# Row-tiled q projection, a VectorE maximum and reciprocal, and one set of PSUM banks in a fused linear-attention and MoE kernel

## The chip, the cores and the metric

The kernel runs as one program on one core of a Trainium2 chip. The metric is the device time of one execution in microseconds. The kernel before takes 699.37 us (median of 3 runs, 699.26 to 699.45). The output must match the reference.

## The reference

Linear attention over 8 batches, 8 heads, 576 tokens and a head size of 64, with 128 random features. Its output, 4608 tokens of 512 values, goes through a feed-forward layer with a softmax-weighted unit and a layer norm.

```python
def _attn_ref(q, k, v, w_phi):
    def phi(x):
        proj = np.einsum('bhsd,df->bhsf', x, w_phi)
        proj = proj - np.max(np.abs(proj), axis=-1, keepdims=True)
        return np.concatenate([np.exp(proj), np.exp(-proj)], axis=-1)
    q_p, k_p = (phi(q), phi(k))
    kv = np.einsum('bhsf,bhsd->bhfd', k_p, v)
    z = np.sum(k_p, axis=2)
    num = np.einsum('bhsf,bhfd->bhsd', q_p, kv)
    den = np.einsum('bhsf,bhf->bhs', q_p, z)[..., None] + 1e-06
    return (num / den).astype(np.float32)

def _moe_ref(x, w_in, w_out, g_ln):
    h = x @ w_in
    e = np.exp(h - np.max(h, axis=-1, keepdims=True))
    sm = e / (np.sum(e, axis=-1, keepdims=True) + 1e-09)
    solu = h * sm
    mu = np.mean(solu, axis=-1, keepdims=True)
    var = np.mean((solu - mu) ** 2, axis=-1, keepdims=True)
    ln = (solu - mu) / np.sqrt(var + 1e-06) * g_ln
    return (ln @ w_out).astype(np.float32)
```

## The kernel before

**Units.** The attention runs in 16 units, one for each batch and each half of the heads (`u`, two units to a batch). A unit has two halves (`sub`), each a pair of heads `j` = 0, 1. For a half the kernel projects k to features (`pjk`), takes the row maximum (`m`), subtracts it (`dk`), takes both exponentials (`ek`) and accumulates keys times values into one PSUM bank (`kv`, 40 matmuls). The features of q come out with features on partitions, in fp32 as `fq`. `num` (36 matmuls) multiplies them with `kv`, and ScalarE copies the result, numerator and denominator together, into `E`. `den_recip` (line 741) and `divide` finish the half with `rc`, `xn` and `xm` on GpSimd.

**q.** Units 0 to 2 project q plainly in fp32 (`pjq`, then transposes `dT`). The other 13 units, 26 halves, take the path that the change rewrites. `q_load` (line 632) loads q of a pair with its 64 rows twice, so that 128 partitions hold it twice (576 KB). `q_hi` rounds all of it to the fast fp32 format on ScalarE, and `q_lo` lets GpSimd overwrite the lower 64 partitions with the rounding remainder, so that one 128-row operand `hq` holds the high part above the low part. `q_proj` (line 644) projects a head and a chunk (320 or 256 tokens) with two full-height matmuls, one with the high weights in both halves (`w_hh`) and one with the low weights above zeros (`w_l0`). A half has four such steps. VectorE transposes each result in blocks of 32 (`blk`), and `q_max4` takes the maximum over 32 features. The maximum over the four partition groups then goes round the engines: a PE transpose (`mtp`), a VectorE maximum (`mt`), a GpSimd copy (`mb`), a PE transpose back (`mcp`), a ScalarE copy (`mcol`). GpSimd subtracts it (`blk<-blk,mcol`), VectorE transposes back into another tile (`pT`) and ScalarE takes the exponentials.

**MoE.** 36 tiles of 128 tokens. For each, a turned copy of the tokens comes through DRAM (`xB`, `dx`, `xT`), is split into high and low (`mxh`, `mxl`), and 24 matmuls fill the two banks of `h`. VectorE takes the maximum (`nm`), ScalarE the exponential, VectorE the product (`eu`), and the result is turned through DRAM (`ub`, `du`, `uTs`), split (`uhs`, `uls`) and multiplied by the output weights (24 matmuls `o`). These weights are unpacked, scaled and centred (`wraw`, `w`, `cms`, `win_l`, `w_out_l`) while the first units run.

**Order.** Every step is one entry of a list, and a table of numbers, `SEQUENCE`, gives the order in which all of them are issued. Each engine carries out its own share strictly in that order. Buffers and PSUM banks are handed out first in, first out along the same order. The eight PSUM banks are three `a` (attention), one `kv`, two for one `h`, and two `mo` (MoE outputs, and `pjk` and `pjq` of early units). From tile 31 on (`TAIL_T`) the attention banks are closed and reopened as a second `h` and two more output banks (`start_tail`, line 1102).

**Where the listing says L263.** The engine wrapper records all instructions at one line, so the profile is read by tile names.

Of the kernel before, what the change touches and what calls it, by code (L numbers as in the profile page):

```python
# [1218 lines left out]
```

## Time and profile before

| what | value |
|---|---|
| median of 3 runs | 699.37 us (699.26 to 699.45) |
| profiled execution, its own time | 699.55 us |
| span of that execution, first to last instruction | 697.8 us |
| mean granted TensorE clock | 0.987 of full speed |
| TensorE (PE) busy | 664.7 us, 95% |
| VectorE (DVE) busy | 472.2 us, 68% |
| GpSimd (POOL) busy | 455.5 us, 65% |
| ScalarE (ACT) busy | 365.1 us, 52% |
| DMA moved | 110.75 MB, 159 GB/s |

PE is the TensorE matmul stream, PEld its weight loads, which lie beside it. Busy time is the union of an engine's instructions. Since matmuls are pipelined, what a matmul costs the stream is the distance from its start to the next one's start, and not its duration. The 1.75 us between span and time lie outside the instructions.

### The profile page before, as it was taken

The page shows a single profiled execution, that of the slowest core. Times are in us where ns is not written, and L with a number is a line of the kernel's source. Part 1 is how long each engine was busy: PE and PEld are TensorE (multiplying, and loading weights), DVE is VectorE, ACT ScalarE, POOL GpSimd, SP SyncE. Part 2 cuts the span into 40 slices and gives each one's busy share as a digit, 9 for nine tenths or more (in the row PEclk, how much of TensorE's full clock was granted, in tenths as well). Part 3 has the DMA queues.
Part 4 walks back from the last instruction along what each step waited for, and adds up shares of the span by engine and source line. Part 5 has one row for each costly group of instructions (what it writes and reads, how often), then busy time and mean ns, then how long its engine had stood idle before and what let it go on. Part 6 is the DMA issues. An engine that isn't in the chain of part 4 may idle for free.

```text
span 697.8 us, 18768 instructions
## 1 busy us (share of the span) xinstructions
PE 664.7 (95%) x7618; PEld 561.0 (80%) x7618; DVE 472.2 (68%) x737; ACT 365.1 (52%) x674; POOL 455.5 (65%) x488
## 2 busy tenths in 40 slices
PE   5968799889999999999999999999999999999998
PEld 4866678778888888888878888888788888788887
DVE  6999788756677786685668577667756773366420
ACT  3967467436564636464656374635644665232232
POOL 1149878986798467766894769754868485553541
PEclk9899899999999999999999999999999999999999
DMA  8954354645465556447544456556555533255342
GB/s 263 355 144 135 90 170 161 150 137 170 128 168 157 173 188 165 147 161 215 179 130 144 96 187 180 154 144 193 165 175 166 173 109 100 71 189 191 104 146 76
DMA packets 109222, 110.75 MB, mean 159 GB/s; under 512 B 46672, under 2 KB 85840, under 8 KB 108624
## 3 DMA queue, kind: packets, MB, share of 16 engines
q1 hardware_dynamic: 109136, 109.55, 51.7%
q8 instruction: 60, 0.98, 0.6%
q14 instruction: 26, 0.21, 0.1%
HBM read 72.29 MB, written 37.22 MB: 157 GB/s over the span
## 4 chain that ended last, share of the span: by engine, by line
PE 73%; POOL 10%; DVE 7%; DMA 4%; issue 2%; SPq 2%; ACT 1%; POOLq 0%; ACTq 0%; DVEq 0%
PE h L263 25%; PE o L263 22%; PE num L263 8%; PE kv L263 8%; PE pjk L263 4%; PE pq L263 4%; DVE w L263 3%; POOL rc L263 3%; POOL hq L263 2%; SPq L263 2%; POOL uls L263 2%; POOL xn L263 1%; DMA rawq<-in_q 1%; DMA wraw<-in_w_in 1%; DVE m L263 1%
## 5 line engine op out<-in xcount | busy, mean ns | idle before, releaser
L263 ACT ACTIVATE ek<-dk 128x512 f32<-128x512 f32 (+1 forms) x160 | 87.6, 585 | 47.8 <-DVE dk L263 47.0
L263 PE MATMUL o<-w_out_h,uhs 128*128 128x512 f32 x280 | 112.3, 401 | 0.0
L263 PE MATMUL o<-w_out_l,uhs 128*128 128x512 f32 x280 | 109.4, 391 | 0.0
L263 PE MATMUL o<-w_out_h,uls 128*128 128x512 f32 x280 | 109.3, 391 | 0.0
L263 POOL TENSOR_TENSOR uls<-uTs,uhs 128x1024 fp32r<-128x1024 f32 x35 | 83.7, 2393 | 31.3 <-ACT uhs L263 23.5
L263 PE MATMUL h<-win_h,mxh 128*128 128x512 f32 x288 | 92.3, 402 | 1.3 <-DVE eu L263 1.2
L263 PE MATMUL h<-win_h,mxl 128*128 128x512 f32 x288 | 89.1, 391 | 0.2 <-POOL mxl L263 0.2
L263 PE MATMUL h<-win_l,mxh 128*128 128x512 f32 x288 | 89.3, 391 | 0.0
L263 POOL TENSOR_TENSOR mxl<-xT,mxh 128x512 fp32r<-128x512 f32 x36 | 46.4, 1289 | 60.6 <-ACT mxh L263 41.9
L263 DVE TENSOR_REDUCE nm<-h 128x1 f32<-128x1024 f32 x36 | 43.8, 1217 | 59.0 <-PE h L263 59.0
L263 POOL TENSOR_TENSOR hq<-rawq,hq 64x1152 fp32r<-64x1152 f32 x26 | 70.5, 2711 | 20.2 <-ACT hq L263 15.4
L263 PEld LDWEIGHTS num<-kvf,fq 128*64 128x64 f32 x2304 | 72.7, 142 | 9.4 <-issue 3.5
L263 PE MATMUL kv<-rv,ek 128*64 128x65 f32 x2048 | 76.9, 222 | 0.8 <-issue 0.8
L263 PE MATMUL num<-kvf,fq 128*64 128x65 f32 x2304 | 77.3, 227 | 0.0
L263 ACT ACTIVATE fq<-pT 128x512 f32<-128x512 f32 (+1 forms) x104 | 66.5, 679 | 19.4 <-DVE pT L263 15.2
L263 DVE STREAM_TRANSPOSE blk<-pq 128x320 f32<-128x320 f32 (+1 forms) x104 | 45.4, 461 | 41.3 <-PE pq L263 37.4
L263 PEld LDWEIGHTS kv<-rv,ek 128*64 128x64 f32 x2048 | 70.9, 138 | 2.2 <-issue 2.2
L263 POOL TENSOR_TENSOR blk<-blk,mcol 128x1152 f32<-128x1152 f32 x26 | 55.5, 2135 | 19.5 <-ACT mcol L263 17.3
L263 ACT ACTIVATE eu<-h,nm 128x1024 f32<-128x1024 f32 x36 | 40.2, 1116 | 51.3 <-DVE nm L263 51.2
L263 DVE TENSOR_REDUCE m<-pjk 128x4 f32<-128x512 f32 (+1 forms) x80 | 48.7, 625 | 24.8 <-PE pjk L263 24.7
L263 PEld LDWEIGHTS h<-win_h,mxl 128*128 128x128 f32 x288 | 53.9, 188 | 12.5 <-POOL mxl L263 0.6
L263 PEld LDWEIGHTS h<-win_l,mxh 128*128 128x128 f32 x288 | 54.1, 188 | 12.0
(93 smaller groups left out, 1326.4 us busy)
## 6 DMA issues: line engine op xcount, KB each, us to landing
du<-ub SPq DMA_DIRECT2D x35, 512.0 KB, 2.9
uTs<-du SPq DMA_DIRECT2D x140, 128.0 KB, 3.3
rawq<-in_q SPq DMA_DIRECT2D x26, 576.0 KB, 4.8
dx<-xB SPq DMA_DIRECT2D x36, 256.0 KB, 2.8
xT<-dx SPq DMA_DIRECT2D x144, 64.0 KB, 2.6
out<-os SPq DMA_DIRECT2D x35, 256.0 KB, 2.8
rawk<-in_k SPq DMA_DIRECT2D x32, 256.0 KB, 3.7
rv<-in_v SPq DMA_DIRECT2D x32, 256.0 KB, 4.1
```

Source lines behind the costliest of these rows:

```text
L263: return self.tc.keep_in_program_order(method(*args, **kwargs))
```

## The change

The q path of the 26 halves is rewritten. q is loaded once (a pair of heads on 128 partitions, 288 KB); high and low parts are two tiles `hq` and `lq`. The projection of a chunk is one step of six matmuls for both heads: three products (high weights with high q, low weights with high q, high weights with low q), each as two matmuls on 64 rows of the array, head 0 on the upper and head 1 on the lower rows, into two banks. The maximum over the partition groups is made by seven small VectorE instructions through one PSUM tile (`far`, named `m4p` in the order). The transposes back are in place. The sum with epsilon moves to ScalarE (`den_eps`), the reciprocal to VectorE. The separate bank sets and the reopening for the tail go: there are five `a` banks, `kv` and one `h`. Buffers of q are regrouped (`qr`, `qh`, `q4`), `xt` has three in place of four. `SEQUENCE` is a new table; its numbers are left out.

```diff
-    rk=3, rkm=2, rv=3, m=4, d=3, e=5, eh=2, kf=2, q4=5, m4=2, mt=2, mb=2, E=2, rc=2,
-    xn=2, xm=2, xt=4, m2k=5, big=8, nm=2, sm=3, bst=2, mv=2, sa=2, sc=3,
+    rk=3, rkm=2, rv=3, m=4, d=3, e=5, eh=2, kf=2, qr=2, qh=4, q4=3, m4=2, E=2, rc=2,
+    xn=2, xm=2, xt=3, m2k=5, big=8, nm=2, sm=3, bst=2, mv=2, sa=2, sc=3,
...
-PSUM_BUFS = dict(a=3, kv=1, h=1, mo=2)
-TAIL_BUFS = dict(th=1, tmo=2)
+PSUM_BUFS = dict(a=5, kv=1, h=1)
...
-        st["rq", sub] = sb("q4", [P, 2, S], name="rawq")
+        st["rq", sub] = sb("qr", [P, S], name="rawq")
...
-        hq = st["hq", sub]
-        hi_lo_sub(nc.gpsimd, hq[D:], st["rq", sub][D:], hq[D:])
-
-    def q_proj(st, sub, j, c):
-        pq = bank("a", [P, 512], "pq")
-        n = QC[c]
-        x = st["hq", sub][:, j, Q0[c] : Q0[c] + n]
-        nc.tensor.matmul(pq[:, :n], lhsT=w_hh, rhs=x, start=True, stop=False)
-        nc.tensor.matmul(pq[:, :n], lhsT=w_l0, rhs=x, start=False, stop=True)
-        st["pq", sub, j, c] = pq
+        st["lq", sub] = sb("qh", [P, S], F32R, "lq")
+        hi_lo_sub(nc.gpsimd, st["lq", sub], st["rq", sub], st["hq", sub])
+
+    def q_proj(st, sub, c):
+        pq = st["pq", sub, c] = two_banks("pq")
+        n, cs = QC[c], slice(Q0[c], Q0[c] + QC[c])
+        hq, lq = st["hq", sub], st["lq", sub]
+        for i, (w, x) in enumerate(((w_hh, hq), (w_ll, hq), (w_hh, lq))):
+            for j, r in enumerate(HEADS):
+                nc.tensor.matmul(pq[j][:, :n], lhsT=w[r, :], rhs=x[r, cs], start=i == 0, stop=i == 2)
...
+        far = bank("a", [P, 512], "m4p")
+        m = st["m4", sub] = sb("m4", [P, NM])
...
+        nc.vector.tensor_copy(out=far[:64, :NM], in_=m[64:])
+        nc.vector.tensor_tensor(out=m[:64], in0=m[:64], in1=far[:64, :NM], op=ALU.max)
+        nc.vector.tensor_copy(out=far[:32, NM : 2 * NM], in_=m[32:64])
+        for q in (3, 2, 1, 0):
+            out = m[32 * q : 32 * q + 32]
+            nc.vector.tensor_tensor(out=out, in0=m[:32], in1=far[:32, NM : 2 * NM], op=ALU.max)
...
-            nc.vector.transpose(out=st["pt", sub][:, j, cs], in_=blk[:, j, cs])
+            nc.vector.transpose(out=blk[:, j, cs], in_=blk[:, j, cs])
...
+    def den_eps(st, sub):
+        st["rc", sub] = sb("rc", [P, 9], name="rc")
+        nc.scalar.activation(out=st["rc", sub], in_=st["E", sub][:, :, 0], func=AF.Copy, bias=EPS)
+
     def den_recip(st, sub):
-        rc = st["rc", sub] = sb("rc", [P, 9], name="rc")
-        nc.gpsimd.tensor_scalar(out=rc, in0=st["E", sub][:, :, 0], scalar1=EPS, scalar2=None, op0=ALU.add)
-        nc.gpsimd.tensor_tensor(out=rc, in0=rc, in1=neg_one, op=ALU.pow)
+        nc.vector.reciprocal(out=st["rc", sub], in_=st["rc", sub])
...
-    def start_tail():
-        nonlocal psa
-        att_stack.close()
-        psa = ctx.enter_context(tc.tile_pool(name="pst", bufs=1, space=PSUM))
```

The order on TensorE behind one visit (`num` and `kv`) in the middle of the program, before. `pq` is the q projection, `mtp` the transpose of the maximum, `h` the first MoE product, `pjk` the projection of k; rows with x2 or x8 are that many matmuls.

```order
L263 MATMUL pq<-hq,w_hh 128x320
L263 MATMUL pq<-hq,w_l_77 128x320
L263 MATMUL mtp<-ident,m_2888 36x128
L263 MATMUL h<-win_h,mxh 128x512 x2
L263 MATMUL h<-win_l,mxh 128x512 x2
L263 MATMUL h<-win_h,mxl 128x512 x2
L263 MATMUL h<-win_h,mxh 128x512 x2
L263 MATMUL h<-win_l,mxh 128x512 x2
L263 MATMUL h<-win_h,mxl 128x512 x2
L263 MATMUL pjk<-wph,rawk 128x128 x8
```

A like place behind a visit in the order after, on the same engine:

```order
L250 MATMUL pq<-hq,w_hh 128x320 x2
L250 MATMUL pq<-hq,w_ll 128x320 x2
L250 MATMUL pq<-lq,w_hh 128x320 x2
L250 MATMUL pjk<-wph,rawk 128x128 x8
L250 MATMUL h<-win_h,mxh 128x512 x2
L250 MATMUL h<-win_l,mxh 128x512 x2
L250 MATMUL h<-win_h,mxl 128x512 x2
L250 MATMUL h<-win_h,mxh 128x512 x2
L250 MATMUL h<-win_l,mxh 128x512 x2
L250 MATMUL h<-win_h,mxl 128x512 x2
```

The projection of a chunk now stands as six matmuls in a row, each row here being the pair for the two heads, and no `mtp` stands in front of `h`.

The order on VectorE around one maximum, before (`m_2888` is the maximum over 32 features, `pT` the transposes back of another half, `ub` and `bst` work of MoE tiles):

```order
L263 BN_AGGR mv<-bst 128x2
L263 TENSOR_REDUCE m_2888<-blk 128x36
L263 STREAM_TRANSPOSE pT<-blk 128x256 x2
L263 TENSOR_REDUCE mt<-mtp 36x32
L263 STREAM_TRANSPOSE ub<-eu 128x8x4x32
L263 TENSOR_REDUCE m<-pjk 128x4 x2
```

And around one maximum after:

```order
L250 TENSOR_REDUCE m_2294<-blk 128x36
L250 COPY m4p<-m_2294 64x36
L250 TENSOR_TENSOR m_2294<-m_2294,m4p 64x36
L250 COPY m4p<-m_2294 32x36
L250 TENSOR_TENSOR m_2294<-m_2294,m4p 32x36 x4
L250 STREAM_TRANSPOSE blk<-pq 128x320
L250 TENSOR_REDUCE nm<-h 128x1
```

The seven small instructions stand in one run behind the large maximum, where before one `mt` came after other work.

The order on GpSimd ahead of the first MoE tile, before, from the fourth division (`rc`, `xn`, `xm`) to the first `mxl`; `win_l` is the low part of the input weights:

```order
L263 TENSOR_SCALAR rc<-E 128x9
L263 TENSOR_TENSOR rc<-rc,neg_one 128x9
L263 TENSOR_TENSOR xn<-E,rc 128x4x128
L263 TENSOR_TENSOR xm<-E,rc 64x64 x2
L263 TENSOR_TENSOR win_l<-w_3_736,win_h 128x1024
L263 TENSOR_TENSOR win_l<-w_0_233,win_h 128x1024
L263 TENSOR_TENSOR win_l<-w_2_1064,win_h 128x1024
L263 TENSOR_TENSOR mxl<-xT,mxh 128x512
```

The same place after:

```order
L250 TENSOR_TENSOR xn<-E,rc 128x4x128
L250 TENSOR_TENSOR xm<-E,rc 64x64 x2
L250 TENSOR_TENSOR win_l<-w_2_959,win_h 128x1024
L250 TENSOR_TENSOR win_l<-w_1_259,win_h 128x1024
L250 TENSOR_TENSOR win_l<-w_3_644,win_h 128x1024
L250 TENSOR_TENSOR mxl<-xT,mxh 128x512
```

The two `rc` rows of the division are gone from GpSimd; three `win_l` and the first `mxl` stand behind the fourth division as before.

## Rows read from the trace of the kernel before

**Rows 1.** The page, part 1: busy us, share of the span, instructions of each engine.

```profile
PE 664.7 (95%) x7618; PEld 561.0 (80%) x7618; DVE 472.2 (68%) x737; ACT 365.1 (52%) x674; POOL 455.5 (65%) x488
```

**Rows 2.** Busy time by stretch: start:end, length, then each engine's busy us; clock, DMA.

```profile
0.00:88.00 88.00, 66.65 (x1140) 56.78 (x1140) 75.74 (x102) 55.47 (x115) 45.15 (x50) 0.90 0.63 196
88.00:188.00 100.00, 95.09 (x1122) 79.56 (x1124) 71.41 (x113) 57.33 (x109) 81.57 (x80) 1.00 0.53 153
188.00:600.00 412.00, 409.70 (x4929) 347.09 (x4924) 281.77 (x468) 224.94 (x410) 290.27 (x307) 1.00 0.53 157
600.00:697.80 97.80, 93.28 (x437) 77.52 (x435) 43.25 (x56) 27.31 (x41) 38.47 (x53) 1.00 0.41 137
```

**Rows 3.** The page, part 4: the chain that ended last, share of the span by engine.

```profile
PE 73%; POOL 10%; DVE 7%; DMA 4%; issue 2%; SPq 2%; ACT 1%; POOLq 0%; ACTq 0%; DVEq 0%
```

**Rows 4.** Timeline of PE, 204 to 212 us: start us, duration us, instruction, count.

```profile
204.47 0.30 PE L263 MATMUL pq<-hq,w_l 128*128 128x320 f32 x1
204.61 0.27 PE L263 MATMUL mtp<-ident,m 128*36 128x128 f32 x1
204.64 0.71 PE L263 MATMUL h<-win_h,mxh 128*128 128x512 f32 x2
205.19 0.62 PE L263 MATMUL h<-win_l,mxh 128*128 128x512 f32 x2
205.64 0.62 PE L263 MATMUL h<-win_h,mxl 128*128 128x512 f32 x2
...
207.00 0.61 PE L263 MATMUL h<-win_h,mxl 128*128 128x512 f32 x2
207.55 1.16 PE L263 MATMUL pjk<-wph,rawk 64*128 64x128 f32 x16
208.64 0.73 PE L263 MATMUL h<-win_h,mxh 128*128 128x512 f32 x2
209.21 0.62 PE L263 MATMUL h<-win_l,mxh 128*128 128x512 f32 x2
...
211.61 0.28 PE L263 MATMUL pq<-hq,w_l 128*128 128x256 f32 x1
211.73 0.27 PE L263 MATMUL mcp<-ident,mb 128*128 128x128 f32 x1
```

**Rows 5.** Groups by line and form: count, busy us, mean ns, idle before.

```profile
L263 PE MATMUL pq<-hq,w_hh 128*128 128x320 f32 x52 | 18.7, 360 | 3.0 <-DVE dk L263 1.8 <-POOL sa L263 1.1
...
L263 PE MATMUL mtp<-ident,m 128*36 128x128 f32 x26 | 7.0, 275 | 1.1 <-DVE dk L263 0.6 <-DVE m L263 0.4
```

**Rows 6.** Timeline of the weight loads (PEld) of that `pjk` at 207.55 us.

```profile
207.55 0.97 PEld L263 LDWEIGHTS pjk<-wph,rawk 64*128 64x128 f32 x16 [0.35 <-issue]
```

**Rows 7.** Groups by line and form of VectorE and GpSimd: count, busy us, mean ns.

```profile
L263 POOL TENSOR_TENSOR hq<-rawq,hq 64x1152 fp32r<-64x1152 f32 x26 | 70.5, 2711 | 20.2 <-ACT hq L263 15.4 <-issue 2.1 <-POOL blk L263 1.3
L263 POOL TENSOR_TENSOR rc<-rc,neg_one 128x9 f32<-128x9 f32 x32 | 59.6, 1861 | 2.7
...
L263 DVE SCALAR_TENSOR_TENSOR w<-wraw,w 128x1024 uint32<-128x1024 uint32 x16 | 24.7, 1549 | 0.1
...
L263 DVE TENSOR_REDUCE mt<-mtp 36x32 f32<-36x128 f32 x26 | 6.8, 260 | 10.3 <-PE mtp L263 10.2
```

**Rows 8.** Timeline of DVE, one of the shortest instructions and the next.

```profile
212.86 0.21 DVE L263 BATCH_NORM_AGGREGATE mv<-bst 128x2 f32<-128x12 f32 x1
212.99 1.17 DVE L263 TENSOR_REDUCE nm<-h 128x1 f32<-128x1024 f32 x1
```

**Rows 9.** Timeline of DVE ahead of the first `h`; in brackets the idle time before.

```profile
76.22 0.71 DVE L263 STREAM_TRANSPOSE xB<-xn 128x512 f32<-128x512 f32 x1 [2.25 <-POOL xn L263]
...
80.57 2.05 DVE L263 SCALAR_TENSOR_TENSOR w<-wraw,w 128x1024 uint32<-128x1024 uint32 x1
```

**Rows 10.** Timeline of PE from the first `h` on.

```profile
88.08 0.70 PE L263 MATMUL h<-win_h,mxh 128*128 128x512 f32 x2
...
96.27 1.50 PE L263 MATMUL warm<-mb 128*128 128x128 f32 x12
```

More of the change, by code (lines that the diff above doesn't have):

```diff
@@ L298, in bank @@
     def bank(tag, shape, name):
-        pool = psa if tag in ("a", "kv", "th", "tmo") else ps
-        return pool.tile(shape, F32, tag=place(tag), bufs=1, name=name)
+        return ps.tile(shape, F32, tag=place(tag), bufs=1, name=name)
     def hi_lo_sub(eng, lo, full, hi):
@@ L309, in linear_attention_then_moe @@
     w_hh = const.tile([P, F], F32R, name="w_hh")
-    w_l0 = const.tile([P, F], F32R, name="w_l0")
-    mb_tiles = [const.tile([P, 4, 32], F32, name=f"mb{i}") for i in range(SBUF_BUFS["mb"])]
+    w_ll = const.tile([P, F], F32R, name="w_ll")
+    zero = const.tile([P, P], F32, name="zero")
     win_h = const.tile([P, DM // P, DF], F32R, name="win_h")
@@ L325, in linear_attention_then_moe @@
     neg_half = work.tile([P, 1], F32, tag="neg_half", bufs=1, name="neg_half")
-    neg_one = work.tile([P, 9], F32, tag="neg_one", bufs=1, name="neg_one")
     make_identity(nc, ident)
     nc = Engines(tc)
-    nc.vector.memset(mb_tiles[0], 0.0)
+    nc.vector.memset(zero, 0.0)
     for t in v_half:
@@ L338, in linear_attention_then_moe @@
     nc.gpsimd.memset(neg_half, -0.5)
-    nc.gpsimd.memset(neg_one, -1.0)
-    nc.gpsimd.memset(w_l0.bitcast(F32), 0.0)
-    for t in mb_tiles[1:]:
-        nc.gpsimd.memset(t, 0.0)
     w_out_tiles = {}
@@ L361, in warm @@
     def warm():
-        z = mb_tiles[0].rearrange("p a b -> p (a b)")
-        w = bank("mo", [P, 512], "warm")
+        w = bank("a", [P, 512], "warm")
         for _ in range(NWARM):
-            nc.tensor.matmul(w[:, :P], lhsT=z, rhs=z, start=True, stop=True)
+            nc.tensor.matmul(w[:, :P], lhsT=zero, rhs=zero, start=True, stop=True)
     def phi_weights():
@@ L428, in w_mean @@
     def w_mean():
-        cm = bank("mo", [P, DM], "cmean")
+        cm = bank("a", [P, DM], "cmean")
         for c in range(2):
@@ L456, in linear_attention_then_moe @@
     op("set", "gpsimd", 1150, -9e4, lambda: None)
-    op("warm", "tensor", NWARM * mm32(P), -1e5, warm, alloc=[("mo", "warm")])
+    op("warm", "tensor", NWARM * mm32(P), -1e5, warm, alloc=[("a", "warm")])
     op("wp", "sync", dma(16 * D * F, True), -40, phi_load)
     op("phi", "scalar", 200, -20, phi_weights, (), ["wp"])
-    op("phil", "vector", 200, -20, phi_weights_lo, after=["phi"])
+    op("phil", "vector", 400, -20, phi_weights_lo, after=["phi"])
     op("gain", "sync", (475, 450), 5, g_load)
@@ L510, in v_half_load, with two_banks @@
         st["vz"] = vz
-    def two_banks(tag, name):
-        if tag == "h":
-            pj = bank(tag, [P, DF], name)
-            return [pj[:, 512 * j : 512 * (j + 1)] for j in range(2)]
-        return [bank(tag, [P, 512], name) for _ in range(2)]
+    def two_banks(name):
+        return [bank("a", [P, 512], name) for _ in range(2)]
     def by_rows(x, pj):
@@ L526, in by_rows, with by_block, k_rows, k_mid @@
                 )
-    def by_block(x, tag, name):
-        pj = bank(tag, [P, 512], name)
+    def by_block(x, name):
+        pj = bank("a", [P, 512], name)
         nc.tensor.matmul(pj[:, : 2 * F], lhsT=x[:, :P], rhs=wph, start=True, stop=True)
         return pj
-    def k_rows(st, g, tag):
-        st["pj", g] = two_banks(tag, "pjk")
+    def k_rows(st, g):
+        st["pj", g] = two_banks("pjk")
         by_rows(st["rk", g], st["pj", g])
-    def k_mid(st, tag):
-        st["pj", 1] = {None: by_block(st["rk", 1], tag, "pjk")}
+    def k_mid(st):
+        st["pj", 1] = {None: by_block(st["rk", 1], "pjk")}
     def row_max(m, pj):
@@ L695, in q_sub @@
         nc.gpsimd.tensor_tensor(
-            out=blk, in0=blk, in1=st["mc", sub].unsqueeze(2).to_broadcast([P, NM, 32]), op=ALU.subtract
+            out=blk, in0=blk, in1=st["m4", sub].unsqueeze(2).to_broadcast([P, NM, 32]), op=ALU.subtract
         )
     def q_back(st, sub, c):
-        if c == 0:
-            st["pt", sub] = sb("q4", [P, 2, S], name="pT")
         blk = st["blk", sub].rearrange("p j b f -> p j (b f)")
@@ L710, in q_exp @@
         nc.scalar.activation(
-            out=st["qf", sub, c][:, :, s, :], in_=st["pt", sub][:, :, Q0[c] : Q0[c] + QC[c]],
+            out=st["qf", sub, c][:, :, s, :], in_=st["blk", sub].rearrange("p j b f -> p j (b f)")[:, :, Q0[c] : Q0[c] + QC[c]],
             func=AF.Exp, scale=1.0 - 2.0 * s,
@@ L791, in add, with banks @@
                [(tag, x[1] if x[0] == "abs" else (u, *x)) for tag, x in alloc], q(tiles), early)
-        def bank_of(tag, g, j):
-            return 0 if tag == "h" or j is None else j
-        def banks(tag, name, g):
-            return [(tag, (name, g, x)) for x in sorted({bank_of(tag, g, j) for j in heads_of(g)})]
+        def banks(name, g):
+            return [("a", (name, g, j)) for j in heads_of(g)]
         heads_of = lambda g: (None,) if g == 1 else (0, 1)
@@ L888, in linear_attention_then_moe @@
-                add(("qmc", sub), "tensor", mm(128), z + 0.7, q_mc, (sub,), [("qmb", sub)], [("a", ("mcp", sub))],
-                    [("mb", sub)])
-                add(("qml", sub), "scalar", 90, z + 0.8, q_mcol, (sub,), [("qmc", sub)], [("m4", ("mc", sub))],
-                    [("mcp", sub)])
-                add(("qs", sub), "gpsimd", 2070, z + 1, q_sub, (sub,), [("qml", sub)], (), [("blk", sub), ("mc", sub)])
+                for c in range(2):
+                    add(("qp", sub, c), "tensor", 3 * (QC[c] / 2.4 + 12), z - 1.2 + 0.4 * c, q_proj, (sub, c),
+                        [("qlo", sub), ("abs", "phil")], [("a", ("pq", sub, c, j)) for j in range(2)],
+                        [("hq", sub), ("lq", sub)])
+                    for j in range(2):
+                        add(("qt", sub, c, j), "vector", dve(QC[c]) + 27, z - 1.0 + 0.4 * c + 0.2 * j, q_turn, (sub, j, c),
+                            [("qp", sub, c)] + prev, () if prev else [("q4", ("blk", sub))],
+                            [("pq", sub, c, j), ("blk", sub)])
+                        prev = [("qt", sub, c, j)]
@@ L893, in linear_attention_then_moe @@
+                add(("qm4", sub), "vector", dve(2 * S) + 800, z, q_max, (sub,), prev,
+                    [("m4", ("m4", sub)), ("a", ("m4p", sub))], [("blk", sub)])
+                add(("qs", sub), "gpsimd", 2070, z + 1, q_sub, (sub,), [("qm4", sub)], (), [("blk", sub), ("m4", sub)])
             for c in range(2):
@@ L900, in linear_attention_then_moe @@
                             [("qe", sub, c, 0)] if s else [("qb", sub, c)], () if s else [("e", ("f", sub, c))],
-                            [("pt", sub), ("f", sub, c)])
+                            [("blk", sub), ("f", sub, c)])
                 else:
@@ L939, in linear_attention_then_moe @@
     M = {}
-    tail = lambda t: t >= TAIL_T
-    turn_tag = lambda t: "q4" if t > LAST else "big"
     def moe_xturn(t):
@@ L971, in moe_lo, with moe_h @@
         hi_lo_sub(nc.gpsimd, lo, M["src", t], hi)
-    def moe_h(t, half, tag):
+    def moe_h(t, half):
         xh, xl = M["xh", t], M["xl", t]
         if half == 0:
-            M["h", t] = bank(tag, [P, DF], "h")
+            M["h", t] = bank("h", [P, DF], "h")
         h = M["h", t]
@@ L1041, in moe_uls, with moe_t @@
         hi_lo_sub(nc.gpsimd, lo, full, hi)
-    def moe_t(t, i, tag):
-        M["uT", t, i] = bank(tag, [P, 4, P], "uT")
+    def moe_t(t, i):
+        M["uT", t, i] = bank("a", [P, 4, P], "uT")
         for c in range(4):
@@ L1062, in moe_o @@
         if half == 0:
-            M["o", t] = bank("mo", [P, DM], "o")
+            M["o", t] = bank("a", [P, DM], "o")
         o = M["o", t]
@@ L1070, in linear_attention_then_moe, with moe_o_last @@
     LAST = 33
-    def moe_o_last(t, half, tag):
+    def moe_o_last(t, half):
         uh, ul = M["uh", t], M["ul", t]
-        o = M["o", t, half] = bank(tag, [P, DM], "o")
+        o = M["o", t, half] = bank("a", [P, DM], "o")
         cs = slice(half * 256, half * 256 + 256)
@@ L1100, in moe_od @@
         nc.sync.dma_start(out=out[t * P : (t + 1) * P, :], in_=M["os", t])
-    def start_tail():
-        nonlocal psa
-        att_stack.close()
-        psa = ctx.enter_context(tc.tile_pool(name="pst", bufs=1, space=PSUM))
-    op("tail", "gpsimd", 0, 2 * B * UNIT + 40, start_tail, (),
-       [(2 * B - 1, "qv", s, c) for s in range(2) for c in range(2)] + [(2 * B - 1, "kve", 1)])
     for t in range(NTOK // P):
@@ L1114, in linear_attention_then_moe @@
         n = lambda k, *a: ("moe", t, k, *a)
-        te = ["tail"] if tail(t) else []
-        h_tag = "th" if tail(t) and t % 2 else "h"
-        u_tag = "tmo" if tail(t) else "mo"
-        e_tag = "e" if tail(t) else "big"
+        e_tag = "e" if t > 30 else "big"
         op(n("xt"), "vector", 640, z - 20, moe_xturn, (t,), dep, [("xt", n("xB"))], xs)
```

126 lines of the change are left out of this document (39 added, 87 removed), and 250 rows, old and new, of the table SEQUENCE.

## The prediction

> **What bounds the kernel now.** I began with the page's first part [rows 1]: TensorE is busy for 664.7 of 697.8 us, so 33 us at most are lost there, and no other engine is over 68%. The stretches [rows 2] tell where. Up to 88 us, just before the first MoE matmul [rows 10], TensorE is busy for 66.65 us and idle for 21.4. VectorE is the fullest engine there, 75.74 of 88 us, because the weights are unpacked there. From 88 to 188 us TensorE idles 4.9 us, from 188 to 600 us 2.3, and after 600 us 4.5, most of it behind the last matmul. The chain [rows 3] agrees: 73% of the span on TensorE, 10% on GpSimd, 7% on VectorE. So from 88 us on an edit is worth what it takes from the matmul stream, unless the stream then waits for VectorE or GpSimd. Before 88 us it is worth what it takes from VectorE's and GpSimd's path to the first `h`.
>
> All sums below are made against the profiled span of 697.8 us. The execution's own time was 699.55 us, 1.75 more; the median of the runs is 0.18 less than that.
>
> **q projection on TensorE: −6.8 us.** What a matmul costs is the distance to the next start. A 320-column step costs 0.14 us (204.47 to 204.61) and a 256-column one 0.12 (211.61 to 211.73) [rows 4]. A half has four of each kind, so 4 × 0.14 + 4 × 0.12 = 1.04 us, and 52 groups like the one in [rows 5] make 26 halves of two chunks and two heads. After, a half has twelve matmuls in six pairs, three pairs for each width. If the two of a pair run at once on the two halves of the array, a pair costs what a single costs now: 3 × 0.14 + 3 × 0.12 = 0.78 us. That saves 0.26 × 26 = 6.8 us. Does a pair run at once? The trace has no 64-row matmul in the fast format, but it has 64-row ones in fp32: `pjk` issues 16 records of 128 columns in 1.09 us (207.55 to 208.64), 0.068 each [rows 4], against at most 1.50 / 12 = 0.125 for the full-height fp32 records of the same size, `warm` [rows 10]. So pairs overlap nearly fully there, and I take that. The other end is no overlap, 2 × 0.78 = 1.56 us a half, which is +0.52 × 26 = +13.5 us (a rival below).
>
> **PE transposes of the maximum gone: −6.2 us.** `mtp` itself moves the next start by only 0.03 us (204.61 to 204.64), but the pair of `h` behind it takes 0.55 us (204.64 to 205.19) where a pair takes 0.45 (205.19 to 205.64) [rows 4]. So one transpose costs 0.12 to 0.13; there are 26 `mtp` [rows 5] and as many `mcp`: 52 × 0.12 = 6.2 us.
>
> **More changes between row-tiled and other matmuls: +2.8 us.** Going from `h` to `pjk` the last pair takes 0.55 us (207.00 to 207.55), 0.10 over 0.45 [rows 4]. The projection now is a 64-row one and so has such joints, where the full-height one had none towards `h` and `o`. Counting every joint between 64-row, 64-column and full matmuls down the two orders gives 136 before and 164 after: 28 × 0.10 = 2.8 us. Several projections stand next to `pjk` or a visit, where a joint exists anyway. The first pair of `h` after `pjk` takes 0.57 us (208.64 to 209.21), another 0.12; if the projection leaves that behind too, it is 28 × 0.22 = 6.2 us. The low end is 0.
>
> **The warm-up moved: −1.3 us.** The six dummy matmuls `warm` stand at 96.27 us, behind the first `h` tile, and take 1.50 us of the stream [rows 10]; 0.1 of that is the overlap with what follows, which I put at −1.3. In the new order they stand ahead of the first visit, where TensorE waits anyway. Cover gone, they cost the same 1.3 again.
>
> **VectorE: +28 us of work, at no cost as long as it is covered.** The trace has no 36-column instruction on VectorE. The nearest are `mv`, whose next instruction starts 0.13 us later (212.86 to 212.99) [rows 8], and `mt`, 0.26 [rows 7]. Seven of them are 0.9 to 1.8 us; I take 0.15 each, near `mv`, which is the smaller and reads what was just written, as these do: 1.05 us, less the 0.18 of the `mt` that goes, × 26 = +23 us. The 32 reciprocals at 0.15 are +5 us. The Trainium skill, VectorE: DVE Perf Modes, section on the TRN2 errata, speaks against this edit: each instruction pays a fixed latency, some 150 cycles as measured there, so many small ones pay it many times. By that, 7 × (150 + 36) / 0.96 GHz = 1.36 us a half, an estimate from the page, and +31 us for the maxima; no row here shows a chain of this kind. What hides the work: VectorE is at 71.41 of 100 us and 281.77 of 412 [rows 2], so it goes to some 76 to 79%. What queues behind the seven are `nm` and `eu`, which free the only `h`, and the transposes `blk`, which free the projection's banks. The tightest place is the stretch from the first `h` to the seventh: adding spacings row by row, the new order holds 79 us of VectorE work against 91 us of matmuls, where the old one holds 68 against 94. I price the extra waiting there and later at +3 us, somewhat under half of what TensorE idles now from 88 to 600 us, 4.9 + 2.3 = 7.2 us [rows 2]. The bounds are −4 (the waits for GpSimd in the next part go, and nothing comes) and +12.
>
> **GpSimd and ScalarE: relief, worth 3 us in the head.** `rc` takes 1.86 us, 32 times, and its addition about 0.3: 70 us go. The remainder of q goes from 2.71 us at 1152 columns [rows 7] to about half that, 26 × 1.3 = 34 us, and `mb` with 7 us. GpSimd falls from 455 to about 345 us. The round trip of a maximum over TensorE, GpSimd and ScalarE no longer exists, so `blk<-blk` on GpSimd waits for VectorE alone. ScalarE loses half of `hq` and `mcol` and gains 32 additions. In the steady part GpSimd was not the bound, and I count its relief inside the +3 above. In the head it was on the path: at 76.22 us VectorE waited 2.25 us for GpSimd's `xn`, which stood behind `rc`, and the last unpacking step took 2.05 us [rows 9] where the mean of its kind is 1.55 [rows 7]. The new order has the same matmuls ahead of the first `h` (53 us by their spacings, both orders) and the same VectorE work (69 and 70 us). So the first `h` comes earlier by what GpSimd held up. I take −3 us; the bounds are −7 (wait and slow steps both gone) and +3 (two more small maxima and reciprocals in the way, keys loaded before queries).
>
> **Banks, tail, loads.** A MoE output now takes one of the five `a` banks that attention uses too; I put that inside the +12 bound. After the last visit the order alternates 24 `h` with 24 `o`. A second `h` bank is then not missed: `nm`, the exponential and `eu` need about 4 us, and 24 `o` last 24 × 0.227 = 5.45. Cover gone, it is 1 us for each of seven tiles. q's halved loads, 26 × 0.29 MB, bound nothing here. All this counts nothing.
>
> **Sum.** −6.8 − 6.2 + 2.8 − 1.3 + 3 − 3 = −11.5 us, a span of 686.3, and 688.0 us with the 1.75 outside. The low end takes −7 for the head, −4 for waits and 0 for joints, in part: about 678. The high end takes +12 for the waits: 697; with some joints at 0.22 it is 699.5.
>
> **The rivals.** *VectorE sets the pace early.* From the first to the seventh `h` VectorE would be at 79 of 91 us, 87%, as dense as in the head (75.74 of 88, 86%), and in the head TensorE lost 24% of its time. If it loses 24% of 91 us there, 22 in place of 4.9, that is +17 in place of +3: 702 us, slower. Against it: in the head TensorE waits for weights and loads too, not for VectorE's density alone. It decides once the seven small instructions cost over 1.8 us together, or an `nm` has to stand behind one chain after another. Chance 0.10.
> *A pair does not run at once.* Then the projection is +13.5 in place of −6.8, and the time is 708 us, slower. The change would not do what it says. For it: the trace shows no such pair in the fast format. Against it: `pjk`. The mechanism could be the weights, since each matmul of a pair loads its own. The loads of `pjk` came 16 in 0.97 us, 0.061 each [rows 6], two in a 0.12 us pair, so there is no room to spare. The Trainium skill, TensorE: Matmul & The Clock Gate, section LDWEIGHTS, says that a load costs its columns over 1.2 GHz, whatever the rows. That is 107 ns for 128 columns, 0.21 us a pair, and with it the six pairs would cost 1.28 us in place of 1.04, +6 us; the trace's 0.061 contradicts it. Chance 0.10.
> *The waits eat the gain.* Old waits stay, new ones for the shared banks come, +12 and more: 698 to 700 us, no change. Chance 0.10.
> *All the waits go.* With GpSimd light the 7.2 us of waits and 7 us of the head vanish: 697.8 − 6.8 − 6.2 + 2.8 − 1.3 − 7.2 − 7 is a span of 672 and a time of 674; I allow half of the way from the forecast, 681 us. Chance 0.08.
>
> **How the numbers follow.** My forecast has the remaining 0.62, and its time is 688.0. The range 678 to 699.5 leaves out the two slower rivals, 0.20. A measurement here can tell 0.2%, 1.4 us, from no change. Faster: 0.62 + 0.08 and 0.04 of the third rival, 0.74. Same: the other 0.06 of it and 0.02 of the first, 0.08. Slower: 0.18.
>
> **What would show it.** Right: `pq` in pairs, two starts within some 0.01 us and 0.12 to 0.14 to the next pair; no `mtp` or `mcp`; `h` behind a projection 0.10 late; TensorE busy some 10 us less; the first `h` at about 85 us; `rc` on VectorE, GpSimd near 345 us. Wrong: `pq` pairs 0.24 apart; small VectorE instructions at 0.26; TensorE idle over 15 us between 88 and 250 us, with VectorE named as what ended it; `o` waiting for an `a` bank.

## The result and the profile after

The changed kernel takes **677.84 us** (median of 4 runs, 676.75 to 679.62) beside 699.41 for the kernel before on the same chip (4 runs, 699.26 to 699.56): a ratio of **0.969, interval 0.967 to 0.972**. The forecast was 688.0, so the direction was right and the size about half: 21.6 us gained in place of 11.4, just under the low end of 678. The profiled execution took 676.75 us, its span is 675.0.

The page's first part after: busy us, share of the span and instructions of each engine, as [rows 1].

```profile
PE 653.6 (97%) x7670; PEld 547.9 (81%) x7670; DVE 497.9 (74%) x926; ACT 350.7 (52%) x680; POOL 347.2 (51%) x395
```

TensorE is busy 11 us less, VectorE 26 us more, GpSimd 108 us less. The stretches, with the columns of [rows 2]:

```profile
0.00:88.00 88.00, 70.24 (x1168) 58.92 (x1169) 79.04 (x117) 56.13 (x119) 35.67 (x39) 0.96 0.66 206
88.00:188.00 100.00, 100.00 (x1266) 83.33 (x1266) 85.56 (x173) 59.68 (x120) 65.07 (x67) 1.00 0.52 149
188.00:600.00 412.00, 412.00 (x4906) 345.63 (x4903) 307.78 (x607) 213.39 (x410) 219.08 (x252) 1.00 0.48 148
600.00:675.00 75.00, 71.41 (x342) 60.02 (x340) 25.51 (x31) 21.51 (x32) 27.37 (x38) 1.00 0.38 121
```

This is the picture to keep: from 88 to 600 us TensorE is busy for 512.00 of 512 us, where it lost 7.2 before [rows 2]. VectorE is fuller there than before (85.56 of the 100 us from 88 to 188, before 71.41) and never makes TensorE wait. The chain that ended last says the same; GpSimd's 10% of [rows 3] are gone from it:

```profile
PE 90%; DVE 5%; issue 1%; ACT 1%; DMA 1%; SPq 0%; ACTq 0%
```

The span divides at the first `h`. It starts at 81.98 us here, at 88.08 before [rows 10]:

```profile
81.98 1.22 PE L250 MATMUL h<-win_h,mxh 128*128 128x512 f32 x2
```

From there to TensorE's last start it is 589.15 us, before 606.14. Following the starts down the stream and taking out every gap in which nothing ran, the idle part is 0.00 us (before 8.35) and the work 589.15 (before 597.79). Behind the last start come 3.8 us (before 3.6). So the span's 22.8 us are: **head −6.1, TensorE's work −8.65, its waits −8.35, end +0.3**.

Now the projection, on TensorE's timeline (start us, duration us, instruction, count), to be read against [rows 4] by the distance from start to start:

```profile
151.53 0.61 PE L250 MATMUL h<-win_h,mxl 128*128 128x512 f32 x2
152.08 0.41 PE L250 MATMUL pq<-hq,w_hh 64*128 64x320 f32 x2
152.33 0.31 PE L250 MATMUL pq<-hq,w_ll 64*128 64x320 f32 x2
152.48 0.31 PE L250 MATMUL pq<-lq,w_hh 64*128 64x320 f32 x2
152.72 0.73 PE L250 MATMUL h<-win_h,mxh 128*128 128x512 f32 x2
153.28 0.62 PE L250 MATMUL h<-win_l,mxh 128*128 128x512 f32 x2
153.75 0.62 PE L250 MATMUL h<-win_h,mxl 128*128 128x512 f32 x2
```

The two of a pair do run at once: the middle pair needs 0.15 us (152.33 to 152.48), and over all halves the distance from pair to pair is 0.145 at 320 columns and 0.117 at 256 (the 0.141 and 0.113 of the expectations below run from a pair's second start to the next pair). But each joint is paid on both sides: the last `h` pair takes 0.55 in place of 0.45 [rows 4], the first `pq` pair 0.25 in place of 0.14; leaving, the last `pq` pair takes 0.24 and the first `h` pair 0.56.

VectorE's new chain for one half, on its timeline:

```profile
219.01 1.34 DVE L250 TENSOR_REDUCE m<-blk 128x36 f32<-128x1152 f32 x1
220.38 0.19 DVE L250 COPY m4p<-m 64x36 f32<-64x36 f32 x1
220.61 0.18 DVE L250 TENSOR_TENSOR m<-m,m4p 64x36 f32<-64x36 f32 x1
220.83 0.19 DVE L250 COPY m4p<-m 32x36 f32<-32x36 f32 x1
221.05 0.79 DVE L250 TENSOR_TENSOR m<-m,m4p 32x36 f32<-32x36 f32 x4
221.77 0.40 DVE L250 TENSOR_REDUCE m<-pjk 128x2 f32<-128x256 f32 x1
```

Seven small instructions take 1.39 us from 220.38 to 221.77, and 1.39 is the median of the 26 halves. I had priced them at 1.05. And the groups that answer to [rows 7] (busy us, mean ns | idle before): the remainder of q on GpSimd costs half, the reciprocal is small, and the unpacking step in the head is shorter, 1333 ns where it took 1549.

```profile
L250 POOL TENSOR_TENSOR lq<-rawq,hq 128x576 fp32r<-128x576 f32 x26 | 37.5, 1446 | 13.5 <-ACT hq L250 8.3 <-PE o L250 3.6 <-PE pq L250 1.3
```

```profile
L250 DVE SCALAR_TENSOR_TENSOR w<-wraw,w 128x1024 uint32<-128x1024 uint32 x16 | 21.2, 1333 | 0.0
...
L250 DVE RECIPROCAL rc<-rc 128x9 f32<-128x9 f32 x32 | 6.2, 194 | 9.5 <-ACT rc L250 9.4
```

### The profile page after: what moved, and what is told of

It is laid out like the page before. It is cut to its first block, busy times and chain, and to the rows that moved or that the text cites. A ratio compares the mean times of both kernels' runs of the same rounds, so it can differ in the third digit from the quotient of the medians.

```text
span 675.0 us, 18936 instructions
## 1 busy us (share of the span) xinstructions
PE 653.6 (97%) x7670; PEld 547.9 (81%) x7670; DVE 497.9 (74%) x926; ACT 350.7 (52%) x680; POOL 347.2 (51%) x395
## 4 chain that ended last, share of the span: by engine, by line
PE 90%; DVE 5%; issue 1%; ACT 1%; DMA 1%; SPq 0%; ACTq 0%
PE h L250 31%; PE o L250 30%; PE kv L250 10%; PE num L250 9%; PE pjk L250 6%; PE pq L250 4%; DVE w L250 3%; DVE m L250 1%; DVE dk L250 1%; PE dT L250 1%; DMA rawq<-in_q 1%; DVE dq L250 1%; PE pjq L250 1%; ACT fq L250 0%; DMA wph<-in_w_phi 0%
## 5 line engine op out<-in xcount | busy, mean ns | idle before, releaser
L250 POOL TENSOR_TENSOR uls<-uTs,uhs 128x1024 fp32r<-128x1024 f32 x35 | 83.8, 2394 | 87.1 <-ACT uhs L250 48.8
L250 ACT ACTIVATE ek<-dk 128x512 f32<-128x512 f32 (+1 forms) x160 | 89.1, 590 | 28.4 <-DVE dk L250 24.4
L250 PE MATMUL h<-win_h,mxh 128*128 128x512 f32 x288 | 95.8, 414 | 0.0
L250 POOL TENSOR_TENSOR blk<-blk,m 128x1152 f32<-128x1152 f32 x26 | 55.4, 2133 | 49.0 <-DVE m L250 48.8
L250 ACT ACTIVATE fq<-blk 128x640 f32<-128x640 f32 (+1 forms) x104 | 67.5, 678 | 21.3 <-DVE blk L250 14.6
L250 PEld LDWEIGHTS num<-kvf,fq 128*64 128x64 f32 x2304 | 69.8, 137 | 10.4 <-issue 7.1
L250 PE MATMUL num<-kvf,fq 128*64 128x65 f32 x2304 | 74.3, 223 | 0.0
L250 PEld LDWEIGHTS o<-w_out_h,uhs 128*128 128x128 f32 x280 | 52.6, 188 | 12.5 <-issue 0.8
L250 PEld LDWEIGHTS h<-win_h,mxh 128*128 128x128 f32 x288 | 51.5, 190 | 13.5 <-issue 1.4
```

Source lines behind the costliest of these rows:

```text
L250: return self.tc.keep_in_program_order(method(*args, **kwargs))
```

## The experiments

The question was where the waits went, since I had expected them to grow. **Theory W**: the moved work took them away by itself, through GpSimd's relief and the shorter way of the maximum. **Theory O** (in later runs F): the new order did it, and the moved work is worth little by itself. The table gives what they came to; "idle" is TensorE's behind the first `h`, of the profiled execution. Runs named `a_` start from the kernel after, `b_` from the kernel before. The kernel before stood at 699.34 to 699.69 beside them.

| run | us | ratio to before, interval | first h | idle |
|---|---|---|---|---|
| before | 699.41 | 1 | 88.1 | 8.35 |
| after | 677.84 | 0.969 (0.967 to 0.972) | 82.0 | 0.00 |
| b_rc | 700.26 | 1.000 (0.998 to 1.002) | 91.8 | 6.45 |
| b_max | 696.55 | 0.996 (0.995 to 0.998) | 89.1 | 9.17 |
| b_rc_max | 703.22 | 1.005 (1.003 to 1.006) | 90.4 | 12.52 |
| a_oldorder | 756.84 | 1.081 (1.078 to 1.085) | 99.5 | 42.68 |
| a_oldorder2 | 747.84 | 1.071 (1.068 to 1.074) | 100.9 | 39.93 |
| a_pool_small | 676.39 | 0.967 (0.965 to 0.969) | 81.1 | 0.22 |
| a_pool_load | 706.77 | 1.011 (1.008 to 1.015) | 86.3 | 18.13 |
| a_rc_pool | 716.97 | 1.024 (1.022 to 1.026) | 89.2 | 21.13 |
| a_chain3 | 735.87 | 1.052 (1.050 to 1.055) | 83.8 | 36.76 |
| a_joined | 709.99 | 1.014 (1.011 to 1.017) | 83.6 | 22.17 |
| a_full | 689.14 | 0.986 (0.984 to 0.989) | 84.4 | 0.00 |
| a_serial | 677.91 | 0.968 (0.966 to 0.970) | 84.8 | 0.00 |

### The moved work in the old order

`b_rc` moves the reciprocal alone:

```diff
-        nc.gpsimd.tensor_scalar(out=rc, in0=st["E", sub][:, :, 0], scalar1=EPS, scalar2=None, op0=ALU.add)
-        nc.gpsimd.tensor_tensor(out=rc, in0=rc, in1=neg_one, op=ALU.pow)
+        nc.scalar.activation(out=rc, in_=st["E", sub][:, :, 0], func=AF.Copy, bias=EPS)
+        nc.vector.reciprocal(out=rc, in_=rc)
```

> The kernel before with the reciprocal alone moved to VectorE, in the old order. Theory W: GpSimd relieved of 70 us, first h some 3 us earlier: 692 to 697 us. Theory F: 698 to 702 us, the first h no earlier than 88 us.

No change, and in the profiled execution the first `h` comes later, not earlier. That execution was the slowest of ten (702.8 us; they spread from 696.95), so the 3.7 us are not a safe number; that nothing was gained is (0.998 to 1.002). Yet GpSimd was relieved as meant: it is busy for 241.29 us between 188 and 600 (before 290.27 [rows 2]).

```profile
88.00:188.00 100.00, 97.73 (x1182) 82.29 (x1180) 73.37 (x122) 59.17 (x117) 75.03 (x72) 1.00 0.55 160
188.00:600.00 412.00, 410.12 (x4939) 347.34 (x4934) 284.87 (x492) 227.74 (x434) 241.29 (x259) 1.00 0.54 157
```

`b_max` takes the maximum over partitions on VectorE, in the step that reduced `mt` before; the steps `mb`, `mc` and `mcol` are empty:

```diff
-        nc.tensor.transpose(out=st["mtp", sub][:NM, :P], in_=st["m4", sub], identity=ident)
...
+        far, m = st["mtp", sub], st["m4", sub]
+        nc.vector.tensor_copy(out=far[:64, :NM], in_=m[64:])
+        nc.vector.tensor_tensor(out=m[:64], in0=m[:64], in1=far[:64, :NM], op=ALU.max)
+        nc.vector.tensor_copy(out=far[:32, NM : 2 * NM], in_=m[32:64])
+        for q in (3, 2, 1, 0):
+            out = m[32 * q : 32 * q + 32]
+            nc.vector.tensor_tensor(out=out, in0=m[:32], in1=far[:32, NM : 2 * NM], op=ALU.max)
```

> The kernel before with the maximum over partitions on VectorE alone (no transposes on TensorE, no GpSimd and ScalarE step), in the old order. Theory W (the edits bring the gain by themselves): 3.85 us of transposes and some waits go: 692 to 696 us. Theory F (an order fitted to its own durations): new waits take the place of what goes, 699 to 705 us.

Faster by 0.4%, between the two theories: near the time of W, but not for W's reason. TensorE's work behind the first `h` falls from 597.79 to 593.71 us, by 4.1 us. The 52 transposes were worth more than that, for after one wait of 2.12 us TensorE ran for a while at the lower of its two clock levels, 1.2 GHz, and an `o` matmul then took 0.43 us from start to start (153.02 to 153.45) in place of 0.24 (156.08 to 156.32):

```profile
152.07 0.46 PE L263 MATMUL pq<-hq,w_hh 128*128 128x320 f32 x1 [2.12 <-POOL sa L263]
...
153.02 0.63 PE L263 MATMUL o<-w_out_l,uhs 128*128 128x512 f32 x1
153.45 0.63 PE L263 MATMUL o<-w_out_h,uls 128*128 128x512 f32 x1
...
156.08 0.40 PE L263 MATMUL o<-w_out_h,uhs 128*128 128x512 f32 x1
156.32 0.40 PE L263 MATMUL o<-w_out_l,uhs 128*128 128x512 f32 x1
```

```profile
150.00:158.00 8.00, 5.93 (x20) 4.84 (x21) 7.73 (x18) 3.87 (x7) 5.13 (x13) 0.79 0.57 164
```

A granted clock of 0.79 over these 8 us costs some 0.21 × 8 = 1.7 us, an estimate; behind the first `h` no other stretch of the two kernels fell, up to the last matmul. So the transposes were worth 5.8 us, 0.11 each. The waits rise by 0.8.

`b_rc_max` has both edits.

> The kernel before, in its own order and with its own banks and full-height projection, with two edits: reciprocal on VectorE, and the maximum over partitions by small VectorE instructions (no transposes on TensorE, no GpSimd and ScalarE step). Theory W: 52 transposes at 0.07 to 0.12 us give 4 to 6 us, most of the 8.35 us of waits and some 3 us of the head go with GpSimd's load: 683 to 687 us. Theory O: only the transposes' 4 to 6 us, less new waits for VectorE: 694 to 697 us, first h near 88 us.

The work is 3.6 us less (it too has a stretch at the lower clock), the waits are 4.2 us more and the head is 2.3 longer: slower by 0.5%, slower even than theory O had it. Its three largest waits of TensorE behind the first `h` (us in total, times, longest) are all for VectorE:

```profile
PE h L263 <- DVE eu L263: 3.1, 2, 2.4
PE pq L263 <- DVE m L263: 2.5, 2, 1.6
PE pq L263 <- DVE dk L263: 1.4, 2, 0.8
```

So theory W falls for these two edits: neither the reciprocal's relief of GpSimd nor the shorter way takes the waits away in an order written for the old steps. The relief by the new projection itself (the remainder of q, 70.5 us of GpSimd before and 37.5 after) is in none of these runs; in the old order it was tried only together with the new banks, below.

### The whole change in the old order

`a_oldorder` is the kernel after with another SEQUENCE: each step at the place of its counterpart before, and where five banks don't suffice, up to 26 places later. `a_oldorder2` does so only up to the last visit and ends in the new order.

> All edits of the change, but its steps stand in the order of the kernel before (a step that finds no free bank is put a few places later). Theory W, the gain comes from the work that was moved (GpSimd relieved, no round trip of the maximum): the order is worth little, 677 to 681 us, TensorE idle under 2 us between 188 and 600 us, first h at 82 to 84 us. Theory O, the new order took away the waits and shortened the head: the 8.35 us of waits behind the first h and the 6.1 us ahead of it come back in large part, 688 to 692 us, first h near 88 us.

> All edits of the change in the order of the kernel before up to the last visit, and behind it in the new order, which needs no second h bank. Where the 757 us of the whole old order came mainly from its last part, written for two h banks: 690 to 705 us. If the old order does not fit the new steps and banks anywhere: over 720 us, TensorE idle over 15 us between 100 and 600 us and the first h at 95 us or later.

Both are far slower than any theory said, and the end of the order is not the reason (757 and 748). TensorE's largest waits in `a_oldorder2` behind the first `h`:

```profile
PE num L247 <- ACT fq L247: 17.7, 5, 16.0
PE h L247 <- DVE eu L247: 9.6, 8, 4.0
```

One wait of 16.0 us of them is where the old order meets the new one. Without it 24 us of idle time and a first `h` at 100.9 us remain. These two runs mix order and banks, since the old order was written for three, two and two banks. The reverse, the new order with the old sets, was not tried: it keeps more than three banks for attention at 564 of its 2330 places and more than two for the MoE at 77, so it cannot be written down with sets of three and two. How much the banks do by themselves stays open.

### What the new order rests on

`a_rc_pool` puts the reciprocal back on GpSimd, as before. `a_pool_load` leaves it on VectorE and adds the same two GpSimd instructions as idle work behind the division:

```diff
+        nc.gpsimd.tensor_scalar(out=spare, in0=neg_one, scalar1=3.0, scalar2=None, op0=ALU.add)
+        nc.gpsimd.tensor_tensor(out=spare, in0=spare, in1=neg_one, op=ALU.pow)
```

> The kernel after with the reciprocal back on GpSimd as an addition and a power, 32 times about 2.1 us, 68 us more for GpSimd. Theory W: the first h comes 2 to 3 us later, and part of the 8.35 us of waits returns: 681 to 686 us. Theory O: GpSimd has room, 677 to 679 us, the same.

> The kernel after, with the addition and the power of the old reciprocal added on GpSimd as idle work behind each division, 32 times about 2.2 us; the real reciprocal stays on VectorE, so the chain from a numerator to its division is as short as in the kernel after, and GpSimd is as loaded as with the reciprocal. Theory L, GpSimd's load is what counts: as slow as with the reciprocal on GpSimd, 710 to 718 us. Theory C, the place in the chain counts: under 685 us.

`a_rc_pool` is 39 us slower than after, far more than I thought, and 29 of them come back with the load alone. So it is mainly GpSimd's load that counts. The other 10 I put down to the place in the chain; `a_rc_pool` also takes the reciprocal off VectorE and the sum off ScalarE, so this is argued and not shown. Of TensorE's 18.1 us of waits in `a_pool_load`, 13.4 are for what queues on GpSimd, the remainders `uls` and `lq`:

```profile
PE o L250 <- POOL uls L250: 7.7, 4, 5.9
PE pq L250 <- POOL lq L250: 5.7, 3, 3.1
```

`a_pool_small` keeps only the small one of the two, 32 times 0.33 us from start to start.

> The kernel after with only the small one of the two idle GpSimd instructions behind each division, 32 times 0.33 us, 11 us in place of some 70. If every microsecond of GpSimd counts in proportion (72 us gave +29), +4 us: 681 to 683 us. If the order leaves GpSimd slack of that size, 677 to 679.5 us.

The same as after: the order has room for these 11 us on GpSimd and not for 72. In busy time, where overlaps count once, the two runs add 7 and 66 us to GpSimd's 347.2.

`a_chain3` does the same for VectorE: `for _ in range(3):` around the seven small instructions.

> The kernel after with the seven small VectorE instructions of the maximum done three times over, two chains more of about 0.95 us for each of 26 halves: +49 us for VectorE, 498 to 547 us of busy time, and 1.9 us more in the chain of every half. If VectorE has the slack that I priced (its new work covered), 677 to 680 us. If the order is as tight for VectorE as the idle GpSimd work showed it to be for GpSimd (72 us gave +29), +15 to +30 us: 693 to 708 us, with waits of TensorE for blk and eu of VectorE.

The three chains take 4.36 us in place of 1.39, so the maxima take 77 us more of VectorE's time, not 49, and the kernel became 58 us slower. The largest waits are for VectorE, as the second theory had it, though for `m` and not for `blk` and `eu`, and the loss is about twice its upper end:

```profile
PE pjk L250 <- DVE m L250: 10.1, 5, 5.2
PE pq L250 <- DVE m L250: 7.0, 7, 2.1
```

`a_joined` changes nothing but the order: 14 places where `h` or `o` steps stood between two row-tiled steps are closed up.

> The kernel after in an order with fewer joints between row-tiled and other matmuls: 14 places where steps of h or o stood between two row-tiled steps are closed up, 164 joints become 140; nothing else moves by more than 34 places of the program. If a joint costs the 0.091 us of the spacings and no wait returns, 24 x 0.091 = -2.2 us: 675 to 676.5 us. If the moved steps bring waits back, 678 us or more, with TensorE idle over 1 us between 100 and 600 us.

It is 32 us slower than after: the second theory holds, at a size that I had not thought of. 22 us of waits came back, the largest for `dk` and `blk`, the readers that free the shared banks:

```profile
PE o L248 <- DVE dk L248: 8.0, 3, 5.2
PE pq L248 <- DVE blk L248: 5.3, 5, 1.7
```

This is the cleanest sign for the order, since the work of every engine is the same: moves of at most 34 places cost more than the whole change brought. It has the five shared banks too, so the banks alone don't keep the waits away.

### The projection by itself

`a_full` multiplies full-height, with zeros in the weights for the other head:

```diff
-                nc.tensor.matmul(pq[j][:, :n], lhsT=w[r, :], rhs=x[r, cs], start=i == 0, stop=i == 2)
+                nc.tensor.matmul(pq[j][:, :n], lhsT=w[:, j * F : (j + 1) * F], rhs=x[:, cs], start=i == 0, stop=i == 2)
```

> The kernel after with the projection full-height: weights with zeros for the other head, so six full-height matmuls a chunk in place of three pairs of 64 rows; the order is untouched (the warm-up reads the identity to free space). Theory P, what the pairs are worth is the work of half the matmuls: a half takes 6 x 0.14 + 6 x 0.12 = 1.56 us in place of 3 x 0.141 + 3 x 0.113 = 0.76, +0.80 x 26 = +21 us, less 33 joints (164 to 131) at 0.091 us, -3 us: 695 to 697 us. Theory F, the order is so fitted to the durations that any longer step lets waits return: over 700 us, with TensorE idle over 5 us between 82 and 600 us.

The pairs are worth 11.3 us, not 17 to 19: `pq` takes 15.4 us more, and with the joints gone `h` and `o` take 5.9 us less and `pjk` 3.1 more. No wait returns (theory F falls here): a longer TensorE step gives the other engines more time, and the order stands that. In its timeline two full-height matmuls take 0.29 us where the pair took 0.15, and there is no joint to `h` (0.29 from the last pair to it):

```profile
155.90 0.45 PE L250 MATMUL pq<-hq,w_hh 128*128 128x320 f32 x2
156.19 0.46 PE L250 MATMUL pq<-hq,w_ll 128*128 128x320 f32 x2
156.48 0.46 PE L250 MATMUL pq<-lq,w_hh 128*128 128x320 f32 x2
156.77 0.63 PE L250 MATMUL h<-win_h,mxh 128*128 128x512 f32 x2
```

`a_serial` has the two loops of the projection exchanged, three matmuls of one head and then three of the other:

```diff
-        for i, (w, x) in enumerate(((w_hh, hq), (w_ll, hq), (w_hh, lq))):
-            for j, r in enumerate(HEADS):
+        for j, r in enumerate(HEADS):
+            for i, (w, x) in enumerate(((w_hh, hq), (w_ll, hq), (w_hh, lq))):
```

> The kernel after with the six projection matmuls of a chunk in another order: three of one head, then three of the other, so that neighbours use the same rows. If the two of a pair do run at once, as the spacing of 0.113 and 0.141 us a pair says, a half takes six times 0.113 and 0.141 in place of three: +0.76 us a half, 26 halves, +20 us: 697 to 699 us, as slow as the kernel before. If the pairs gain nothing by standing beside each other, the same 677 to 679 us.

No difference, and so it doesn't test the overlap: the trace shows the same pairs again, at the same distances (0.145 and 0.117).

```profile
153.23 0.42 PE L250 MATMUL pq<-hq,w_hh 64*128 64x320 f32 x2
153.49 0.31 PE L250 MATMUL pq<-hq,w_ll 64*128 64x320 f32 x2
153.63 0.32 PE L250 MATMUL pq<-lq,w_hh 64*128 64x320 f32 x2
153.88 0.73 PE L250 MATMUL h<-win_h,mxh 128*128 128x512 f32 x2
```

## Why the prediction was right in direction and half in size

**The step that failed is the waits.** I wrote +3 us; they were −8.35. The span gained 11.3 us more than the forecast, and this term is 11.35 of them; the other misses nearly cancel. I reached +3 from VectorE's density and put GpSimd's relief inside it, because "In the steady part GpSimd was not the bound". As a statement on the kernel before it holds: `b_rc` relieves GpSimd and gains nothing. It doesn't hold for the kernel after: with the reciprocal's load back on GpSimd, 18 to 21 us of waits return. What I missed is that the order is a term of its own. I went through it for the tight places and asked how much worse it might become, not whether it had been written for the relieved engines and could use the room that the old order let lie. Neither half does it alone: the moved work in the old order gives −0.4 to +0.5%, the new order with the reciprocal's load on GpSimd +1.1 to +2.4%. The new order with all of the old work was not run, so for the rest of the moved work the same is argued, not shown.

**The rival *All the waits go* is what happened**, and I gave it 0.08. Its full working gave 674 us, of which I allowed only half, 681; the measured 677.84 lies between. Its reason, a light GpSimd, is half of the cause: without the order it brought nothing in `b_rc`. *VectorE sets the pace early* didn't come: VectorE is at 85.56 of 100 us and TensorE has no idle time. But `a_chain3` shows that it stood near: 3 us more in each half cost 58 us. *A pair does not run at once* is excluded by 0.145 and 0.117 us a pair.

**TensorE's work: −11.5 forecast, −8.65 measured.** Part of the gap is the clock. In the kernel after the granted clock is 0.79 from 80 to 88 us, and the first `h` pair takes 1.22 us where it took 0.70 [rows 10]. `a_serial` and `a_pool_small`, at 1.00 there, have 587.65 and 587.45 us of work, 10.1 and 10.3 less than before. The transposes were sized nearly right: 6.2 forecast, 5.8 by `b_max` at the full clock. The warm-up was −1.3 and is −1.39. What remains, projection with joints, is about −3.0 against −6.8 + 2.8 = −4.0. The pairs came as sized, 0.145 and 0.117 us against 0.14 and 0.12. The joints are the mis-sized part: one costs 0.1 us on each of its sides, 0.2 in all, which I had only as the bound. With it the prediction's sum would be −6.8 + 28 × 0.2 = −1.2. Some 2 us of the −3.0 are old waits that are counted as work (last section). The rest of this balance, `pjk`'s time among it (3.5 us less), I did not separate.

**VectorE's work** was undersized, and it did not matter: 1.39 us a half in place of 1.05, because the seven start 0.20 to 0.23 us apart where I took 0.15. I took it that these distances come from reading what was just written; but three of the last four don't read what the one before wrote, and they start 0.20 to 0.22 apart too. What sets the distance stays open. The Trainium skill, VectorE: DVE Perf Modes, section on the TRN2 errata, speaks of a fixed price for each instruction; the prediction's estimate from it, 1.36 us, was the better one, and this trace agrees with it.

**The head: −3 forecast, −6.1 in the profiled execution**, −3 to −7 over the kernels with nearly the same head (first `h` at 81.1 to 84.8), so single profiles differ by some 4 us here. The reason I gave, GpSimd's relief, is at most a part of it: in the old order the relief brings the first `h` no earlier (89.1 to 91.8), in the new order loading GpSimd again makes it later (86.3, which is little beyond that spread, and 89.2). Banks, tail and loads show no loss, as forecast: behind the last start there are 3.8 us in place of 3.6, and no `o` waits in the kernel after.

## What to carry to other kernels

A fixed order is fitted to the lengths of its steps: here moving work off an engine freed room that only an order written for it turned into time, so price the pair of edit and order, and read the order for what it no longer waits for, not for its tight places alone. With TensorE the bound and never idle, this order stood longer TensorE steps (`a_full`), and broke when the engines that feed it got slower or the same steps were shuffled a little. Judge an experiment that puts an edit into a foreign order as one on the fit, not on the edit.

## What the chip showed that I had not expected

- **A wait costs more than its own length.** In `a_chain3` TensorE idled 36.8 us behind the first `h`, and the way from there to its last start grew by 56.3; in `a_joined` 22.2 and 32.3. The matmuls themselves got slower: the granted clock is 0.98 between 188 and 600 us, where it is 1.00 after. It falls behind waits: from 138 us on TensorE was busy for 1.35 of 6 us, and the next 7 us ran at 0.52, near the lower level of 1.2 GHz.

```profile
138.00:144.00 6.00, 1.35 (x32) 1.02 (x28) 5.33 (x25) 1.07 (x3) 0.00 (x0) 1.00 0.00 0
144.00:151.00 7.00, 5.95 (x28) 5.00 (x29) 4.86 (x13) 0.00 (x0) 5.58 (x6) 0.52 0.24 77
```

From the two stretches below, the lower clock costs at most 0.03 × 100 + 0.02 × 412 = 11 us, an estimate, of the 19.5 us by which the way grew beyond the waits; in `a_joined`, at 0.98 in both stretches, some 10 of 10.1. The rest in `a_chain3` is in part a matter of counting: a wait counts from the end of the last matmul, which lasts some 0.39 us, where the next would have started 0.23 behind it. That leaves out 0.16 us a wait, some 6 us for its 39 waits, and some 2 us for the 14 of the kernel before.

```profile
88.00:188.00 100.00, 90.99 (x1098) 74.80 (x1097) 87.68 (x234) 50.58 (x102) 57.37 (x57) 0.97 0.45 126
188.00:600.00 412.00, 384.24 (x4495) 317.45 (x4492) 337.94 (x849) 198.78 (x384) 196.04 (x224) 0.98 0.46 136
```

- **Matmuls on different rows started out of the program's order** in `a_serial`: the first matmuls of the two heads, first and fourth in the program, started 0.010 us apart, and both 0.24 ahead of the heads' second ones (in the kernel after, where the two stand side by side in the program, they started 0.003 apart). The Trainium skill, TensorE: Matmul & The Clock Gate, Part 3 on packing small matmuls, says that matmuls start in the order of the program; this trace shows pairs where the program has threes. Whether TensorE's queue did it or a step between the program and the chip, no row tells.
- **A joint between 64-row and full matmuls costs 0.2 us**, 0.1 on each side. The Trainium skill, TensorEngine Tiling (Array Packing), section Key Properties, says that a change of the tiling mode drains TensorE first, without a figure; a cost on both sides of each change agrees with it, though no row here shows the drain itself.
